# Summing wrapped spectra by accumulating transfers into DRAM, and one doubling step by accumulating transfers into SBUF, in a two-layer SSM and SwiGLU kernel

## The chip, the cores and the metric

The kernel runs on one core of a Trainium2 chip. The metric is the device time of one launch in microseconds: 1188.11 us, median of three runs. The engines are written as in the profile: PE (TensorE matmul), PEld (its weight loads), DVE (VectorE), ACT (ScalarE), POOL (GpSimd) and SP (SyncE, which here only issues transfers). Each engine works through its own queue in order.

## The reference, cut to what matters

One sequence of 2048 rows and 512 channels passes twice through an S4 convolution layer and a SwiGLU layer, each on the layer-normed input and added back.

```python
logdA = dt * A                                   # A complex [512, 128], dt = exp(log_dt)
P = jnp.exp(logdA[:, :, None] * l[None, None, :])            # 128 complex powers for 2048 lags
K = jnp.einsum("dn,dnl,dn->dl", Cc, P, dB).real              # the convolution kernel [512, 2048]
Kf = rfft(pad(K, 2048)); Uf = rfft(pad(u, 2048))
y  = irfft(Uf * Kf)[:2048] + u * Dskip

x = x + ssm(layernorm(x)); x = x + ((silu(n @ w_gate) * (n @ w_up)) @ w_down)   # twice; n = layernorm(x)
```

## The kernel before

The program has three stages.

**The kernel of the convolution** (0 to about 310 us). The 512 channels go in eight chunks of 64. For a chunk, the lag is split in two digits. `gen_g` makes `g`, the coefficients C·dt·B times the powers 0 to 31, real and imaginary in `g[:, 0]` and `g[:, 1]`, by doubling: powers 1 to 3, then 4 to 7 from 0 to 3, 8 to 15 from 0 to 7, 16 to 31 from 0 to 15. A doubling is a complex product: two DVE products into `g` and a scratch tile (`tm`, named `btl` in the profile; `th_`, named `tmp`) and a sum of them. For 4 and 8 the sums are DVE subtractions and additions (L488, L489). For 16 they are transfers that POOL issues and that add into SBUF (`accum_op=OP.add`, L494 and L499). `gen_turns`, `gen_reduce`, `gen_trig` (phases and sines: L365, L385, L388 on DVE, L376, L382, L395 to L397 on ACT), `gen_exp` and `gen_mags` (magnitudes) and `gen_e` (their products: L450 to L459 on DVE) make the other digit's table `re`, `im` of the chunk after the next. `lags` contracts both on PE (L509, L510) into `pk`, ACT copies it to `ks` (L515), `spread` turns it on PE into `kp` (L525), ACT copies that to `kt` (L1001), and `spectra` transforms `kt` on PE (L546) for four frequency classes `q` in the order 0, 3, 1, 2 and four blocks `k` of 512 lags. Between them PE sums squares of the weight matrices (L320, from ACT's L316).

In `spectra`, the spectrum of block k wraps into block k+1 by a turn of ±90 degrees, so what is stored for k = 1 to 3 is s[i, k] ± s[1−i, k−1], with i the real or imaginary part. ACT copies the product out of PSUM (`s1`, L555), POOL copies block 0 to `w0r` (L557) and makes the two sums (`wo`, L563), and SP writes three blocks to DRAM (`wdr`, L569). For the last three classes blocks 1 to 3 are made later than block 0 (L566, L567), after the work that starts the next stage.

**The hand-over** (about 310 to 350 us): the first convolution block is finished on DVE, its norm goes over POOL (L204 to L207), ACT and PE, the last three spectra are made, the weights are split into two halves of fp16 (ACT L626, DVE L632, L654) and the first SwiGLU matmuls start.

**The blocks** (to the end): eight blocks of 512 rows, each a convolution (DVE L736 and L739, which read `w` from `wdr` and `uu` from `udr`; PE L270, L755) and a SwiGLU (PE L860 to L862, L874 to L876).

In the first stage and the hand-over up to the second convolution block, PE, DVE and ACT run in the order in which the program is written: generators of instructions are advanced one step at a time by `take(generator, steps)`, and the numbers in these calls set the order. The queues of POOL and SP, and everything after that, are ordered by a scheduler when the program is built. Buffers come from named pools; the tag `uu` has three buffers and holds `s1`, the `u` of the second block and `uu`; the tag `sg` has two and holds `wo` and later the SwiGLU's `sg`.

Of the kernel before, what the change touches and what calls it, by code (L numbers as in the profile page):

```python
# [15 lines left out]
AF = mybir.ActivationFunctionType  # L16
OP = mybir.AluOpType
# [5 lines left out]
P = 128  # L23
T = 512
NB = L // T
# [9 lines left out]
DC = 64  # L35
# [46 lines left out]
def kernel(ctx, tc, x, a_re, a_im, b_re, b_im, c_re, c_im, log_dt, d_skip,  # L82
                           w_gate, w_up, w_down, c_ef, c_ei, c_ek, c_am, c_eh, c_eih, out):
    nc = tc.nc
# [10 lines left out]
    def tl(shape, name, tag, dt=F32):  # L95
        return sb.tile(shape, dt, name=name, tag=tag, bufs=BUFS[tag])
# [365 lines left out]
    def gen_g(ch, ts, g):  # L462

        re, im, mu, xz, mz, t16 = ts
        w_ = w0[:, :, ch * DC:(ch + 1) * DC]
        for t in xz:
            V.tensor_tensor(t, t, mz, OP.mult)
        yield
        tm, th_ = tmp
        V.tensor_tensor(g[:, :, 0], w_, re[:, :, 64].unsqueeze(1).to_broadcast([P, 2, DC]), OP.mult)  # L470
        V.tensor_tensor(tm[:, :, 0], w_[:, ::-1], im[:, :, 64].unsqueeze(1).to_broadcast([P, 2, DC]), OP.mult)
        yield
        V.tensor_tensor(g[:, 0, 0], g[:, 0, 0], tm[:, 0, 0], OP.subtract)
        V.tensor_tensor(g[:, 1, 0], g[:, 1, 0], tm[:, 1, 0], OP.add)
        yield
        zr, zi = (t[:, :3].unsqueeze(1).to_broadcast([P, 2, 3, DC]) for t in xz)
        V.tensor_tensor(g[:, :, 1:4], g[:, :, 0:1].to_broadcast([P, 2, 3, DC]), zr, OP.mult)
        V.tensor_tensor(tm[:, :, :3], g[:, ::-1, 0:1].to_broadcast([P, 2, 3, DC]), zi, OP.mult)
        yield
        V.tensor_tensor(g[:, 0, 1:4], g[:, 0, 1:4], tm[:, 0, :3], OP.subtract)  # L480
        V.tensor_tensor(g[:, 1, 1:4], g[:, 1, 1:4], tm[:, 1, :3], OP.add)
        for n in (4, 8):
            yield
            zr, zi = (t[:, ZP.index(n)].unsqueeze(1).unsqueeze(1).to_broadcast([P, 2, n, DC]) for t in xz)
            V.tensor_tensor(g[:, :, n:2 * n], g[:, :, 0:n], zr, OP.mult)
            V.tensor_tensor(tm[:, :, :n], g[:, ::-1, 0:n], zi, OP.mult)
            yield
            V.tensor_tensor(g[:, 0, n:2 * n], g[:, 0, n:2 * n], tm[:, 0, :n], OP.subtract)  # L488
            V.tensor_tensor(g[:, 1, n:2 * n], g[:, 1, n:2 * n], tm[:, 1, :n], OP.add)  # L489
        yield  # L490
        zr, zi = (t[:, NZ - 1:].to_broadcast([P, 16, DC]) for t in xz)
        V.tensor_tensor(g[:, 1, 16:], g[:, 1, :16], zr, OP.mult)
        V.tensor_tensor(th_, g[:, 0, :16], zi, OP.mult)
        G.dma_start(g[:, 1, 16:], th_, accum_op=OP.add)  # L494
        yield
        tl_ = tm.rearrange("p i s d -> p (i s) d")
        V.tensor_tensor(g[:, 0, 16:], g[:, 0, :16], zr, OP.mult)
        V.scalar_tensor_tensor(tl_, g[:, 1, :16], -1.0, zi, OP.mult, OP.mult)
        G.dma_start(g[:, 0, 16:], tl_, accum_op=OP.add)  # L499
        yield  # L500
# [30 lines left out]
    def spectra(ch, kt, k0, k1, qs=QORD):  # L531
# [4 lines left out]
        for q in qs:  # L536
# [6 lines left out]
            for i, c in [(i, c) for c in range(4) for i in range(2)] if k1 == 1 else \  # L543
# [3 lines left out]
                if k0 == 1 and (i, c) == (0, 3):  # L547
                    yield
            yield
            if k1 == 1:  # L550
                A.activation(w0r[:, h, q, :, off:off + DC].rearrange("p i (g d) -> p i g d", g=4), pw[:, :, 0], AF.Copy)
                yield
                continue
            s1 = tl([P, 2, NB, 4, 16], "s1", "uu")
            A.activation(s1[:, :, :nk], pw, AF.Copy)  # L555
            if k0 == 0:
                G.tensor_copy(w0r[:, h, q, :, off:off + DC].rearrange("p i (g d) -> p i g d", g=4), s1[:, :, 0])  # L557
            sp, np_ = s1, NB - 1
            wo = tl([P, 2, NB - 1, 4, 16], "wo", "sg")
            ops = (OP.subtract, OP.add) if q % 2 == 0 else (OP.add, OP.subtract)  # L560
            for i in range(2):
                if k0 == 0:
                    G.tensor_tensor(wo[:, i], s1[:, i, 1:], s1[:, 1 - i, :3], ops[i])  # L563
                else:
                    w0s = w0r[:, h, q, 1 - i, off:off + DC].rearrange("p (g d) -> p g d", g=4)
                    G.tensor_tensor(wo[:, i, 0], s1[:, i, 0], w0s, ops[i])  # L566
                    G.tensor_tensor(wo[:, i, 1:], s1[:, i, 1:3], s1[:, 1 - i, :2], ops[i])  # L567
            for k in range(1, NB):
                nc.sync.dma_start(wdr[k, h, q, :, :, off:off + DC].rearrange("p i (g d) -> p i g d", g=4),  # L569
                                  wo[:, :, k - 1])  # L570
            yield


    def sizes(ch, kt, junk):

# [19 lines left out]
    def take(it, n):  # L595
        for _ in range(n):
            next(it, None)
# [301 lines left out]
    with tc.manual_schedule(engines={mybir.EngineType.Activation, mybir.EngineType.DVE, mybir.EngineType.PE}):  # L899
# [58 lines left out]
        for i in range(NCH - 1):  # L958
# [24 lines left out]
            if more:  # L983
                rd = gen_reduce(ts[i + 2])
                next(rd)
            for g in (gg, gg, ge, gg, ge, gg, gg, rd, rd, ge, rd, rd, ge, rd, rd, rd, rd):
                take(g, 1)
            while tops:
                tops.pop(0)()
# [3 lines left out]
            if more:  # L993
                f = second(*sec[i])
                next(f)
            take(gg, 2)
            if more:
                tr = gen_trig(ts[i + 2])
                take(tr, 1)
# [93 lines left out]
        take(rest, 3)  # L1093
        take(second(*sec[-1], space=pbig), 2)
        take(rest, 100)
        split(1, 0)
        take(first, 1)
        split(0, 1)
# [47 lines left out]
```

## Time and profile before

| | |
|---|---|
| median of three runs | 1188.11 us (1188.05 to 1190.89) |
| the profiled execution, its own time | 1194.56 us |
| its span, first to last instruction | 1192.8 us |
| PE busy | 1108.3 us (93%) |
| DVE busy | 1026.5 us (86%) |
| ACT busy | 618.0 us (52%) |
| POOL busy | 185.0 us (16%) |
| mean granted TensorE clock | 0.983 |

A busy share over the whole span mixes the three stages. In the first stage POOL is far from idle and PE, DVE and ACT are all close to full; in the last, PE and DVE are. The program has one core, so there is one row of clock and span.

### The profile page before, as it was taken

The numbers are of one execution on the slowest core, as the hardware profiler recorded it, in microseconds if no ns is written. First come the engines' busy times: TensorE is split into PE (matmuls) and PEld (weight loads), VectorE is DVE, ScalarE is ACT, GpSimd is POOL, SyncE is SP. The second block draws the span as 40 slices with busy tenths as digits, with TensorE's granted clock in tenths as the row PEclk, the third lists the DMA queues.
The fourth block names the chain that finished last, engine by engine and source line by source line (L and its number), as shares of the span: only waits on it lengthen the run. The fifth ranks groups of instructions, "written<-read, shape, count | busy, mean of one in ns | idle before, by whom it ended". The sixth has DMA issues, their size and how long they took to land.

```text
span 1192.8 us, 25266 instructions
## 1 busy us (share of the span) xinstructions
PE 1108.3 (93%) x10268; PEld 861.2 (72%) x10268; DVE 1026.5 (86%) x1621; ACT 618.0 (52%) x1166; POOL 185.0 (16%) x238
## 2 busy tenths in 40 slices
PE   2889999889887989999999999999999999999998
PEld 2767776667875767768677787868687686867875
DVE  7989999997879999999999999999992899983211
ACT  6998887862355544537743523655432553224211
POOL 3105454343310011202100000211000010000000
PEclk9989999999989999999999999999999999999999
DMA  6444445577497326432344354324434134312000
GB/s 234 141 107 127 114 119 127 126 181 201 141 297 221 109 89 163 161 111 89 85 152 146 115 165 142 111 81 150 140 123 133 45 115 128 125 46 45 15 23 18
DMA packets 139031, 147.95 MB, mean 124 GB/s; under 512 B 77921, under 2 KB 87137, under 8 KB 138914
## 3 DMA queue, kind: packets, MB, share of 16 engines
q1 hardware_dynamic: 134050, 129.56, 35.8%
q0 software_dynamic: 4864, 16.78, 5.9%
q8 instruction: 80, 1.31, 0.5%
q14 instruction: 37, 0.30, 0.1%
HBM read 99.24 MB, written 28.31 MB: 107 GB/s over the span
## 4 chain that ended last, share of the span: by engine, by line
PE 35%; DVE 26%; issue 5%; ACT 3%; DMA 2%; POOL 2%; SPq 1%; DVEq 0%; ACTq 0%; POOLq 0%
PE pgu L860 6%; PE pgu L861 6%; PE pgu L862 6%; DVE t L736 4%; PE py L874 4%; PE py L875 4%; PE py L876 3%; DVE yk L739 3%; DVE yk L736 3%; PE pi L755 3%; PE pf L270 2%; DVE z L226 2%; DVE sg L866 2%; POOL rs L221 2%; DVE bt L226 1%
## 5 line engine op out<-in xcount | busy, mean ns | idle before, releaser
L860 PE MATMUL pgu<-mix,wsl 128*128 128x256 f16 x1280 | 350.2, 274 | 5.3 <-DVE sg L866 3.6
L862 PE MATMUL pgu<-mix,wsl 128*128 128x256 f16 x1280 | 350.3, 274 | 3.6 <-DVE wsl L632 3.6
L861 PE MATMUL pgu<-mix,wsl 128*128 128x256 f16 x1280 | 350.2, 274 | 0.0
L874 PE MATMUL py<-wsl,hh 128*128 128x512 f16 (+1 forms) x352 | 135.5, 385 | 8.9 <-DVE sgr L836 3.1
L861 PEld LDWEIGHTS <-wsl 128*128 128x128 f16 x1280 | 125.7, 98 | 21.8 <-issue 5.8
L862 PEld LDWEIGHTS <-wsl 128*128 128x128 f16 x1280 | 125.7, 98 | 19.1 <-DVE wsl L632 3.9
L860 PEld LDWEIGHTS <-wsl 128*128 128x128 f16 x1280 | 125.7, 98 | 15.8
L876 PE MATMUL py<-wsl,hl 128*128 128x512 f16 (+1 forms) x352 | 135.2, 384 | 1.3 <-DVE hl L868 1.3
L865 ACT ACTIVATE sg<-pgu,sc 128x512 f32<-128x512 f32 x80 | 54.5, 682 | 135.4 <-PE pgu L862 116.5
L736 DVE TENSOR_TENSOR t<-uu,w 128x1024 f32<-128x1024 f32 x96 | 117.0, 1219 | 8.2 <-DMA uu<-udr 7.9
L875 PE MATMUL py<-wsl,hh 128*128 128x512 f16 x320 | 123.3, 385 | 0.0
L739 DVE TENSOR_TENSOR yk<-yk,t 128x1024 f32<-128x1024 f32 x96 | 116.9, 1218 | 0.2
L866 DVE SCALAR_TENSOR_TENSOR sg<-pgu,sc,sg 128x512 f32<-128x512 f32 x80 | 59.7, 746 | 51.0 <-ACT sg L865 50.8
L546 PE MATMUL pw<-kt,ek 128*128 128x256 f32 (+2 forms) x420 | 98.6, 373 | 0.0
L755 PE MATMUL pi<-yl,mix 128*128 128x256 f16 x672 | 91.4, 273 | 1.7 <-ACT yl L744 1.4
L546 PEld LDWEIGHTS pw<-kt,ek 128*128 128x128 f32 x420 | 78.7, 195 | 9.5
L867 ACT ACTIVATE hh<-sg 128x512 f16<-128x512 f32 x80 | 50.0, 625 | 57.5 <-DVE sg L866 57.4
L221 POOL TENSOR_TENSOR rs<-mv,mhalf 128x2 f32<-128x2 f32 (+1 forms) x21 | 38.3, 1824 | 263.2 <-ACT mv L220 255.8
L270 PE MATMUL pf<-z,eh 128*128 128x256 f16 x576 | 74.6, 273 | 1.4 <-ACT z L260 1.4
L755 PEld LDWEIGHTS <-mix 128*128 128x128 f16 x672 | 65.2, 98 | 13.0 <-issue 2.0
L736 DVE TENSOR_TENSOR yk<-u,w0r 128x1024 f32<-128x1024 f32 x56 | 68.2, 1218 | 0.3 <-ACT u L272 0.3
L875 PEld LDWEIGHTS <-hh 128*128 128x128 f16 (+1 forms) x352 | 34.8, 99 | 46.2 <-issue 11.7
(240 smaller groups left out, 2245.8 us busy)
## 6 DMA issues: line engine op xcount, KB each, us to landing
w<-wdr SPq DMA_DIRECT2D x96, 256.0 KB, 2.7
uu<-udr SPq DMA_DIRECT2D x96, 256.0 KB, 3.0
udr<-u POOLq DMA_DIRECT2D x32, 256.0 KB, 2.9
wdr<-wo SPq DMA_DIRECT2D x96, 64.0 KB, 2.5
udr<-u SPq DMA_DIRECT2D x16, 256.0 KB, 2.2
g<-tmp POOLq DMA_DIRECT2D x8, 512.0 KB, 4.5
g<-btl POOLq DMA_DIRECT2D x8, 512.0 KB, 5.9
n<-ndr SPq DMA_DIRECT2D x16, 256.0 KB, 3.0
```

The lines of the kernel that those rows point to most:

```text
L270: PE.matmul(pf[:, o], lhsT=e, rhs=m, start=k == 0, stop=k == len(terms) - 1)
L546: PE.matmul(pw[:, i], lhsT=e, rhs=kt[:, :, c + 4 * k0:4 * k1:4, :].rearrange("p g k d -> p k g d"), start=c == 0, stop=c == 3)
L736: V.tensor_tensor(t, uu.unsqueeze(1).to_broadcast([P, 2, 2, HD]), w.unsqueeze(2).to_broadcast([P, 2, 2, HD]), OP.mult)
L739: V.tensor_tensor(yk, yk, t, OP.add)
L755: PE.matmul(pi[:, o], lhsT=e, rhs=m, start=k == 0, stop=k == len(terms) - 1)
L860: PE.matmul(o, lhsT=wgu(wi, k, 0)[:, fs], rhs=nh[:, k], start=k == 0, stop=False)
L861: PE.matmul(o, lhsT=wgu(wi, k, 0)[:, fs], rhs=nlo[:, k], start=False, stop=False)
L862: PE.matmul(o, lhsT=wgu(wi, k, 1)[:, fs], rhs=nh[:, k], start=False, stop=k == 3)
L866: V.scalar_tensor_tensor(sg, pgu[:, 1], sc6[:, 4:5], sg, OP.mult, OP.mult)
L874: PE.matmul(py[:, r], lhsT=hh[:n, f, rc], rhs=wd(f, 0)[:n], start=f == 0, stop=False)
L875: PE.matmul(py[:, r], lhsT=hh[:n, f, rc], rhs=wd(f, 1)[:n], start=False, stop=False)
L876: PE.matmul(py[:, r], lhsT=hl[:n, f, rc], rhs=wd(f, 0)[:n], start=False, stop=f == FT - 1)
```

## The change

Four edits.

1. In `gen_g` the step from 8 to 16 powers loses its two DVE sums. Its two DVE products of 1024 elements become four of 512, one of them with a factor −1, and two transfers issued by POOL add the second products into `g` (L488, L491 of the changed kernel).
2. In `spectra`, POOL computes nothing. ACT writes a negated copy `ng` of one part (L572, or L570 from `s1`) beside `s1`. SP copies block 0 from `s1` to `w0r` (L573) and writes the unwrapped blocks 1 to 3 of both parts to `wdr` (two transfers, L576). Then POOL issues two transfers that add `ng` and `s1`, one block further, into the same places of `wdr` (L585, L586). They are put in the program one class later, by `wrapped(1)`; each has to wait until the plain write of its place has landed. For the three late classes block 0 is copied back from `w0r` by ACT (L569).
3. The `take` order of a chunk: the doubling to 16 powers now stands before the phase reduction, one step of `gen_e` behind it, and the last doubling before `spread` instead of behind it.
4. Behind the last spectra stands `wrapped()`, for the last two additions.

`ng` takes the place of `wo` in tag `sg` (two buffers). `s1` is now also read by the second addition, so its buffer comes free later.

The diff:

```diff
@@ gen_g
         for n in (4, 8):
             yield
             zr, zi = (t[:, ZP.index(n)].unsqueeze(1).unsqueeze(1).to_broadcast([P, 2, n, DC]) for t in xz)
+            if n == 8:
+                V.tensor_tensor(g[:, 1, 8:16], g[:, 1, :8], zr[:, 1], OP.mult)
+                V.tensor_tensor(tm[:, 1], g[:, 0, :8], zi[:, 1], OP.mult)
+                G.dma_start(g[:, 1, 8:16], tm[:, 1], accum_op=OP.add)
+                V.tensor_tensor(g[:, 0, 8:16], g[:, 0, :8], zr[:, 0], OP.mult)
+                V.scalar_tensor_tensor(tm[:, 0], g[:, 1, :8], -1.0, zi[:, 0], OP.mult, OP.mult)
+                G.dma_start(g[:, 0, 8:16], tm[:, 0], accum_op=OP.add)
+                continue
             V.tensor_tensor(g[:, :, n:2 * n], g[:, :, 0:n], zr, OP.mult)
             V.tensor_tensor(tm[:, :, :n], g[:, ::-1, 0:n], zi, OP.mult)
@@ spectra
+            w0s = w0r[:, h, q, :, off:off + DC]
+            wrapped(1)
             if k1 == 1:
-                A.activation(w0r[:, h, q, :, off:off + DC].rearrange("p i (g d) -> p i g d", g=4), pw[:, :, 0], AF.Copy)
+                A.activation(w0s.rearrange("p i (g d) -> p i g d", g=4), pw[:, :, 0], AF.Copy)
                 yield
                 continue
-            s1 = tl([P, 2, NB, 4, 16], "s1", "uu")
-            A.activation(s1[:, :, :nk], pw, AF.Copy)
-            if k0 == 0:
-                G.tensor_copy(w0r[:, h, q, :, off:off + DC].rearrange("p i (g d) -> p i g d", g=4), s1[:, :, 0])
-            wo = tl([P, 2, NB - 1, 4, 16], "wo", "sg")
-            ops = (OP.subtract, OP.add) if q % 2 == 0 else (OP.add, OP.subtract)
+            s1 = tl([P, 2, NB, DC], "s1", "uu")
+            ng = tl([P, NB - 1, DC], "ng", "sg")
+            j = q % 2
+            A.activation(s1[:, :, k0:].rearrange("p i k (g d) -> p i k g d", g=4), pw, AF.Copy)
+            if k0:
+                A.activation(s1[:, :, 0], w0s, AF.Copy)
+                A.activation(ng, s1[:, 1 - j, :3], AF.Copy, scale=-1.0)
+            else:
+                A.activation(ng.rearrange("p k (g d) -> p k g d", g=4), pw[:, 1 - j, :3], AF.Copy, scale=-1.0)
+                nc.sync.dma_start(w0s, s1[:, :, 0])
+            to = wdr[1:, h, q, :, :, off:off + DC].rearrange("k p i d -> p i k d")
             for i in range(2):
-                (the sums on POOL: L563, or L566 and L567)
-            for k in range(1, NB):
-                nc.sync.dma_start(wdr[k, h, q, :, :, off:off + DC].rearrange("p i (g d) -> p i g d", g=4),
-                                  wo[:, :, k - 1])
+                nc.sync.dma_start(to[:, i], s1[:, i, 1:])
+            wraps.append((to[:, j], ng, to[:, 1 - j], s1[:, j, :3]))
             yield
 
+    wraps = []
+
+    def wrapped(keep=0):
+        while len(wraps) > keep:
+            t0, f0, t1, f1 = wraps.pop(0)
+            G.dma_start(t0, f0, accum_op=OP.add)
+            G.dma_start(t1, f1, accum_op=OP.add)
@@ the loop over chunks
-            for g in (gg, gg, ge, gg, ge, gg, gg, rd, rd, ge, rd, rd, ge, rd, rd, rd, rd):
+            for g in (gg, gg, ge, gg, gg, gg, gg, rd, rd, ge, rd, rd, ge, rd, rd, rd, rd, ge):
                 take(g, 1)
...
-            take(gg, 2)
@@ the hand-over
         take(rest, 100)
+        wrapped()
```

The change moves instructions at three places that matter below. The first is DVE in the middle of a chunk: the doubling to 16 powers, the doubling to 32 behind it, and the phase reduction (L388) and the products of `gen_e` (L450, L453). Before:

```order
L453 TENSOR_TENSOR re<-re 128x4x8x32
L388 SCALAR_TENSOR_TENSOR im<-t_1333,re 128x64x2
L388 SCALAR_TENSOR_TENSOR im<-t_1333,re 128x64 x2
L485 TENSOR_TENSOR g<-g,xr 128x2x512
L486 TENSOR_TENSOR btl<-g,xi 128x1024
L488 TENSOR_TENSOR g<-g,btl 128x512
L489 TENSOR_TENSOR g<-g,btl 128x512
L492 TENSOR_TENSOR g<-g,xr 128x1024
```

And with the change, in the same chunk:

```order
L490 SCALAR_TENSOR_TENSOR btl<-g,xi 128x512
L385 TENSOR_TENSOR xi<-xi,xr 128x384
L388 SCALAR_TENSOR_TENSOR im<-t_1335,re 128x64x16
L450 TENSOR_TENSOR im<-im,re 128x4x8x32
L388 SCALAR_TENSOR_TENSOR im<-t_1335,re 128x64x8
L388 SCALAR_TENSOR_TENSOR im<-t_1335,re 128x64x4
L453 TENSOR_TENSOR re<-re 128x4x8x32
L388 SCALAR_TENSOR_TENSOR im<-t_1335,re 128x64x2
L388 SCALAR_TENSOR_TENSOR im<-t_1335,re 128x64 x2
L453 TENSOR_TENSOR re<-re 128x4x8x32
L500 TENSOR_TENSOR g<-g,xr 128x1024
```

L490 is the last of the four products of the step to 16 powers and L500 the first reader of what the two transfers add. The step moved ahead of the phase reduction, which stands, with an L450 and two L453, between the two. In the first chunk only one L388 stands there.

The second is POOL at the hand-over, where L204 to L207 are the norm of the first SwiGLU block. Before:

```order
L567 TENSOR_TENSOR wo<-s_3349 128x128
L566 TENSOR_TENSOR wo<-s_3349,w0r 128x64
L567 TENSOR_TENSOR wo<-s_3349 128x128
L204 TENSOR_SCALAR rs<-mv 128x2
L205 TENSOR_TENSOR rs<-rs,mhalf 128x2
```

And with the change:

```order
L586 DMA wdr<-s_3248 128x3x64
L585 DMA wdr<-ng 128x3x64 x2
L586 DMA wdr<-s_3363 128x3x64
L204 TENSOR_SCALAR rs<-mv 128x2
L205 TENSOR_TENSOR rs<-rs,mhalf 128x2
```

Where the sums of one class stood ahead of L204, there are now two transfers of that class (the second L585 and the last L586), each of which waits for the landing of a plain write.

The third is DVE right after it: L632 (L646 with the change) makes the low halves of the weights, L736 (L750) is the first product of the second convolution block and needs `uu`, L222 is the norm of the next rows and needs a POOL result. Before:

```order
L632 SCALAR_TENSOR_TENSOR wsl_3093<-xg,sc_93,wsl_3092 128x2x344
L736 TENSOR_TENSOR t<-uu,w 128x1024
L632 SCALAR_TENSOR_TENSOR wsl_3094<-st_3470,sc_93,wsl_3093 128x4x344
L739 TENSOR_TENSOR yk<-yk,t 128x1024
L632 SCALAR_TENSOR_TENSOR wsl_3092<-st_3483,sc_93,wsl_3092 128x2x344
L632 SCALAR_TENSOR_TENSOR wsl_3093<-st_3483,sc_93,wsl_3092 128x2x344
L632 SCALAR_TENSOR_TENSOR wsl_3094<-st_3487,sc_93,wsl_3093 128x4x344
```

And with the change:

```order
L646 SCALAR_TENSOR_TENSOR wsl_3105<-xg,sc_93,wsl_3104 128x2x344
L646 SCALAR_TENSOR_TENSOR wsl_3106<-st_3483,sc_93,wsl_3105 128x4x344
L646 SCALAR_TENSOR_TENSOR wsl_3104<-st_3496,sc_93,wsl_3104 128x2x344
L646 SCALAR_TENSOR_TENSOR wsl_3105<-st_3496,sc_93,wsl_3104 128x2x344
L222 SCALAR_TENSOR_TENSOR rs<-mv,rs 128x2
L646 SCALAR_TENSOR_TENSOR wsl_3106<-st_3500,sc_93,wsl_3105 128x4x344
L750 TENSOR_TENSOR t<-uu,w 128x1024
```

The first read of `uu` moved behind four of these weight instructions and behind L222. On PE the order up to the hand-over is the same as before.

7 lines of the change are left out of this document (removed).

## The prediction

> **What bounds the kernel now.** The removed work lies in the first 345 us, so I read that stage first: busy time by stretches cut at ACT's `ks` (L515), which begins each chunk's turn.
>
> ```profile
> core 0: us, PE busy (x) PEld busy (x) DVE busy (x) ACT busy (x) POOL busy (x), PEclk, DMA share, GB/s
> 98.88:130.27 31.39, 28.37 (x391) 21.75 (x390) 30.46 (x38) 26.46 (x43) 13.65 (x19) 1.00 0.56 132
> 161.30:193.96 32.66, 29.75 (x391) 23.08 (x390) 32.52 (x40) 26.20 (x44) 16.09 (x20) 0.95 0.56 138
> ```
>
> DVE is busy for 97% of the one turn and 99.6% of the other, which looks like the bound. The waits over the five turns from 98.88 to 256.34 (total, times, longest) say otherwise:
>
> ```profile
> ACT ks L515 <- PE pk L510: 15.4, 5, 3.5
> PE nrm L320 <- ACT sq L316: 8.3, 5, 1.7
> DVE xi L385 <- ACT xr L376: 0.4, 1, 0.4
> ```
>
> ACT and PE wait for each other once in every turn; neither waits for DVE, and DVE waits for ACT. One turn in order of time, ACT and then PE:
>
> ```profile
> 193.96 1.02 ACT L515 ACTIVATE ks<-pk 128x1024 f32<-128x1024 f32 x1 [2.98 <-PE pk L510]
> 199.00 0.57 ACT L555 ACTIVATE s<-pw 128x512 f32<-128x512 f32 x1
> 213.31 1.23 ACT L316 ACTIVATE sq<-st 128x344 bf16<-128x344 f32 x3
> 213.83 1.07 PE L320 MATMUL nrm<-sq,onesb 128*128 128x344 bf16 x3 [1.64 <-ACT sq L316]
> 225.38 1.03 ACT L515 ACTIVATE ks<-pk 128x1024 f32<-128x1024 f32 x1 [3.49 <-PE pk L510]
> ```
>
> From `ks` to the first `sq` ACT shows no idle time (193.96 to 213.31, 19.4 us); from `nrm` to the end of the lag products PE waits for nothing but its own issue (213.83 to 225.38, 11.5 us); then `ks` again. That loop of ACT and PE is the 31.4 us of the turn, and no DVE instruction is in it. DVE keeps pace beside it. Behind the first stage the picture turns:
>
> ```profile
> 346.00:360.00 14.00, 14.00 (x112) 11.75 (x111) 14.00 (x21) 8.92 (x13) 0.00 (x0) 0.85 1.04 320
> 400.00:500.00 100.00, 94.69 (x791) 74.81 (x790) 98.29 (x169) 54.94 (x108) 14.62 (x13) 0.98 0.45 135
> ```
>
> There DVE is full and PE has gaps, so what DVE loses or gains at the hand-over is kept.
>
> **The change part by part.** The sum is made as a difference in the profiled execution (1194.56 us, span 1192.8) and put on the median, 1188.11, which is 6.4 lower; every term is a stretch of well under 10 us, so the half per cent between the two doesn't touch it.
>
> *DVE relief, in the turns.* Mean nanoseconds over the five turns, then two undisturbed records from the quiet start:
>
> ```profile
> L485 DVE TENSOR_TENSOR g<-g,xr 128x1024 f32<-128x1024 f32 x5 | 6.5, 1296 | 0.0
> L485 DVE TENSOR_TENSOR g<-g,xr 128x512 f32<-128x512 f32 x5 | 3.5, 699 | 0.0
> L488 DVE TENSOR_TENSOR g<-g,btl 128x512 f32<-128x512 f32 x5 | 3.5, 692 | 0.2
> L489 DVE TENSOR_TENSOR g<-g,btl 128x512 f32<-128x512 f32 x5 | 3.4, 684 | 0.0
> L467 DVE TENSOR_TENSOR xi<-xi,mzp 128x384 f32<-128x384 f32 x5 | 4.4, 875 | 0.0
> L450 DVE TENSOR_TENSOR im<-im,re 128x1024 f32<-128x1024 f32 x10 | 13.9, 1394 | 0.0
> 25.73 0.55 DVE L467 TENSOR_TENSOR xi<-xi,mzp 128x384 f32<-128x384 f32 x1
> 31.86 1.22 DVE L450 TENSOR_TENSOR im<-im,re 128x1024 f32<-128x1024 f32 x1
> ```
>
> Two sums go (0.69 + 0.68 = 1.38), two products of 1.3 become four of 0.70 (+0.2): DVE saves 1.2 us a turn. With POOL's sums gone the stretched instructions shrink as well; these two lines alone give 0.33 + 2 × 0.17 = 0.7 us a turn. Ten to fifteen us of DVE time go in all. I price this at **0**: the cover is the loop of ACT and PE. If that were not the bound, it would be worth up to PE's wait of 1.7 us a turn (first rival). The Trainium skill, page "SBUF — State Buffer", section "Who interferes with whom", says that a DVE instruction with two SBUF inputs contends with a GpSimd instruction that reads SBUF, and that PE and ACT never wait on anyone; the stretched rows agree with the first half, and by the second half the loop gets nothing from a silent POOL, so the sum stays as it is.
>
> *The negated copy on ACT.* No copy of 192 elements from PSUM is in the trace; the nearest are
>
> ```profile
> L551 ACT ACTIVATE w0r<-pw x3: 277/277/277, 301.4 to 304.9; 128x128 f32<-128x128 f32 x3
> L555 ACT ACTIVATE s<-pw x32: 490/588/610, 88.3 to 330.5; 128x512 f32<-128x512 f32 x29, 128x384 f32<-128x384 f32 x3
> ```
>
> so 0.28 to 0.49, by the slope 0.33, of which neighbouring ACT records overlap by 0.1: 0.23 us. Of the four per turn only the one behind L555 at 199.00 stands between `ks` and `sq`; the other three eat into the wait of 3 us before `ks`. Five turns: **+1.2 us** (bounds 0.9 to 2.5).
>
> *The first chunk.* Here only one L388 stands between the step to 16 powers and L500, and DVE has to wait for two transfers. The nearest prices:
>
> ```profile
> L690 POOL DMA_DIRECT2D udr<-u x32: 539/542/672, 421.9 to 876.2; - x32
> L499 POOL DMA_DIRECT2D g<-btl x8: 861/870/882, 50.9 to 269.8; - x8
> udr<-u POOLq DMA_DIRECT2D x32, 256.0 KB, 2.9
> g<-tmp POOLq DMA_DIRECT2D x8, 512.0 KB, 4.5
> 51.30 1.12 ACT L395 ACTIVATE re<-im 128x1024 f32<-128x1024 f32 x1 [1.06 <-DVE im L388]
> ```
>
> An addition of 256 KB into SBUF should land 2.9 (a plain one of that size) to 4.5 us after its issue; I take 3.5, nearer the plain one. From L490 to L501 DVE has 1.1 + 1.1 us to do, so it waits some 1.8 us in two pieces, less the 1.2 saved: the last L388 comes 0.6 later, and ACT, which waits for it at 51.30 and is full from there, moves with it. **+0.7 us** (0 to 2.5). In later chunks some 7 us stand in between.
>
> *The hand-over.* DVE before:
>
> ```profile
> 341.38 1.22 DVE L736 TENSOR_TENSOR t<-uu,w 128x1024 f32<-128x1024 f32 x1 [7.94 <-DMA uu<-udr]
> 342.52 1.64 DVE L632 SCALAR_TENSOR_TENSOR wsl<-st,sc,wsl 128x1376 f16<-128x1376 f32 x1
> 345.22 3.34 DVE L632 SCALAR_TENSOR_TENSOR wsl<-st,sc,wsl 128x688 f16<-128x688 f32 x3
> 344.22 0.40 PE L862 MATMUL pgu<-mix,wsl 128*128 128x256 f16 x1 [3.62 <-DVE wsl L632]
> 344.00:350.00 6.00, 5.78 (x28) 4.10 (x29) 6.00 (x9) 0.00 (x0) 0.00 (x0) 0.50 1.05 404
> ```
>
> DVE stood for 7.94 us at a load of `uu` with four ready L632 behind it; PE stood 3.62 us for one of them and then ran 6 us at a granted clock of 0.50. With the read of `uu` behind them, the first three can go into the gap. The fourth is behind L222, whose POOL step was at 341.5 to 343.2, so it comes about where the first is now. Against it stands POOL's L204:
>
> ```profile
> 319.48 0.78 POOL L204 TENSOR_SCALAR rs<-mv 128x2 f32<-128x2 f32 x1 [1.99 <-DVE mv L203]
> 314.61 0.49 ACT L555 ACTIVATE s<-pw 128x384 f32<-128x384 f32 x1 [2.49 <-PE pw L546]
> wdr<-wo SPq DMA_DIRECT2D x96, 64.0 KB, 2.5
> ```
>
> It now follows two transfers that wait for plain writes of the copy of 314.61: issued at 315.2 and 316.1, landed 2.5 to 3.2 later, then two POOL issues of about 1.2 (384 rows of 256 B; bounds 0.54, the plain 256 KB, and 1.9): L204 at about 320.8, 1.3 late. DVE by 344: of the four L632, all done with the change instead of one, so 1.64 + 2 × 0.85 = 3.3 us gained, with that delay already in it. **−3.3 us** (bounds −6.6, PE's stall and the half clock with it, to +3 if POOL comes late).
>
> Sum: +1.2 + 0.7 − 3.3 = −1.4: **1186.7 us**.
>
> **The rivals.**
>
> *DVE is the bound after all*: it is over 97% busy, and its one short wait could be noise. Then each turn falls by PE's wait of 1.7 us, over six turns 10 us, and with the hand-over the time is 1176 to 1178. Against it: ACT's rows show no wait for DVE in any of the five turns.
>
> *Slower: the copy buffer.* `ng` has two buffers, and a class needs the buffer of the class before last.
>
> ```profile
> 213.81 2.50 SPq L314 DMA_DIRECT2D st<-in_B_w_up_dram  x3
> 214.44 0.58 ACT L555 ACTIVATE s<-pw 128x512 f32<-128x512 f32 x1
> 220.17 0.59 ACT L555 ACTIVATE s<-pw 128x512 f32<-128x512 f32 x1
> 220.65 1.24 ACT L316 ACTIVATE sq<-st 128x344 bf16<-128x344 f32 x3
> ```
>
> The first class is copied at 214.44; SP is free at 216.3, its first plain write is out at 217.8 and down at 219.4 to 220.3, the addition lands 3.5 later (2.3 to 5.9): 222.9, at worst 226. The third class wants the buffer at 220.7 and ACT then needs 1.24 for `sq` before `ks` at 225.4. So up to 224.1 it is hidden, and each us beyond is one on the loop. It decides from an addition of 4.7 us on. At 5.9, 1.4 us a turn; with PE's longer waits pulling the clock down in some turns (the turn with 0.95 is 1.3 us longer than the one with 1.00), 2 to 2.5: 1188.1 + 5 × 2.2 − 1.4, about 1198. For it: pieces of 256 B, read, added and written in DRAM, of which no row exists. The Trainium skill, "DMA: Bandwidth & Descriptors", section "Specifications", puts line rate at 512 B and above. The rows agree: 64 KB in 256 B pieces took 2.5 us, 256 KB in longer ones 2.9.
>
> *The hand-over gains nothing*: `uu` now sits behind a 768 KB load in SP's queue, L222 behind POOL's transfers; the 3.3 goes to 0 to +3, the time to 1190 to 1193.
>
> *The last stage falls otherwise*: its order is made anew by the scheduler, DVE and PE are both near full, and PE's waits there come in pieces of 1 to 3.5 us; a few of them more or fewer move the end by ±4.
>
> **How the numbers follow.** What this kernel's measurement can tell from no change is 0.3%, 3.6 us: 1184.5 to 1191.7. The forecast with its own bounds (1184 to 1191) 0.45; DVE as the bound 0.15, faster; the copy buffer 0.17, slower; no gain at the hand-over 0.11, half of it slower; the last stage 0.12, half faster and half slower. Out of the forecast's own 0.45, 0.09 lies beyond 3.6 us on the fast side, where PE's half clock goes too. Faster 0.15 + 0.06 + 0.09 = 0.30; slower 0.17 + 0.05 + 0.06 = 0.28; same 0.42. Range 1177 to 1198, from DVE as the bound to the copy buffer.
>
> **What would show it.** Right: turns of 31 to 32 us as before; DVE's idle time up by 2 to 4 us a turn, put down to ACT (L385 waiting for L376); ACT's wait before `ks` shorter by about 1 us, PE's before `nrm` longer by 0.2; in the first chunk DVE waiting at L500 and L501 for transfers; PE without a wait for `wsl` near 342 and full clock there. Wrong: turns under 30.5 us (DVE was the bound); ACT's L572 waiting for a transfer, with `ks` no longer waiting for PE (copy buffer); DVE waiting 5 us or more at L222 or L750.

## The result and the profile after

The changed kernel takes 1217.96 us (median of 6 runs, 1216.51 to 1220.61) against 1190.33 us for the kernel before (6 runs beside it): 1.0237 times as long, 95% interval 1.0219 to 1.0256. The forecast was 1186.7 us with a range of 1177 to 1198, so it is wrong in its sign and its range.

The stages, cut at ACT's `ks` (L515, now L523). "SwiGLU" is the first matmul of L860 (L874). The second profile of the kernel before was taken among the experiments; it matters, because the first one was of a long execution.

| us | before, as quoted in the prediction | before, second profile | changed |
|---|---|---|---|
| its own time | 1194.56 | 1186.43 | 1216.51 |
| first `ks` | 68.65 | 68.26 | 69.31 |
| first to seventh `ks`, six turns | 187.69 | 187.98 | 194.99 |
| seventh turn | 26.16 | 25.78 | 32.15 |
| eighth `ks` to SwiGLU | 51.17 | 48.67 | 52.68 |
| SwiGLU to the end | 859.1 | 853.9 | 865.6 |

Every stage is longer. The turns of the changed kernel, by stretches from `ks` to `ks`:

```profile
core 0: us, PE busy (x) PEld busy (x) DVE busy (x) ACT busy (x) POOL busy (x), PEclk, DMA share, GB/s
100.41:134.82 34.41, 29.72 (x389) 22.50 (x388) 27.23 (x39) 27.48 (x48) 14.54 (x15) 0.95 1.06 165
198.86:230.52 31.66, 28.12 (x391) 21.88 (x390) 27.05 (x39) 27.20 (x49) 14.25 (x14) 1.00 1.09 180
264.30:296.45 32.15, 24.74 (x370) 19.81 (x369) 19.06 (x30) 9.00 (x18) 14.35 (x13) 0.95 1.03 217
```

DVE is indeed relieved: 27 us busy in a turn instead of 31. The turn is not shorter, and where the clock (PEclk) is 0.95 it is longer by 2 to 3 us. The share of the DMA engines went from 0.5 to over 1. The waits up to 345 us (total, times, longest):

```profile
POOL wdr L585 <- DMA wdr<-s: 96.5, 11, 15.2
DVE xi L385 <- ACT xr L376: 20.1, 6, 5.1
ACT ng L572 <- DMA wdr<-ng: 18.6, 6, 8.4
DVE g L500 <- DMA g<-btl: 12.6, 2, 11.1
PE pk L517 <- DMA g<-btl: 10.2, 2, 5.2
```

DVE's new idle time is put down to ACT, as forecast. But ACT waits for a copy buffer, DVE for the step to 16 powers, PE for the last doubling, all of them for transfers that POOL issues; and POOL itself stands 96.5 us before L585, for plain writes of SP. The seventh turn shows how these belong together. DVE, then POOL, PE and ACT:

```profile
259.38 0.69 DVE L487 TENSOR_TENSOR btl<-g,xi 128x512 f32<-128x512 f32 x1
275.79 1.22 DVE L500 TENSOR_TENSOR g<-g,xr 128x1024 f32<-128x1024 f32 x1 [11.11 <-DMA g<-btl]
...
265.69 1.28 POOL L586 DMA_DIRECT2D wdr<-s  x1 [3.96 <-ACT ks L523]
266.48 1.42 POOL L488 DMA_DIRECT2D g<-btl  x1
267.83 2.31 POOL L491 DMA_DIRECT2D g<-btl  x1
278.97 1.28 POOL L585 DMA_DIRECT2D wdr<-ng  x1 [8.83 <-DMA wdr<-s]
...
289.38 0.45 PE L517 MATMUL pk<-re,g 128*32 128x64 f32 x3 [5.05 <-DMA g<-btl]
...
295.60 0.34 ACT L572 ACTIVATE ng<-pw 128x192 f32<-128x192 f32 x1 [8.40 <-DMA wdr<-ng]
```

L488's data were ready at 260.1, but it stands in POOL's queue behind an L586 that waits, and is issued at 266.5, 6.4 us late; then it takes 9.3 us to land. DVE has nothing else to do in this chunk and waits 11.11 us for it. So the last doubling is late too, and PE stands 5.05 us for it. The additions themselves wait for plain writes (8.83 us at one L585), and with them the buffer that ACT needs (8.40 us). For the L586 at 265.69 (and the L585 at 335.09 below) the profile names an instruction of ACT that ended in the same moment; but a plain write of SP landed at 265.14 (334.54), and POOL starts 0.54 to 0.57 us behind such a landing at 25 of the 27 transfers of L585 and L586 that it stood for. At the hand-over the same happens to L204, whose input was ready at 332.9, and PE then stands 5.74 us (3.33 and 2.96 before):

```profile
335.09 1.28 POOL L585 DMA_DIRECT2D wdr<-ng  x1 [12.97 <-ACT s L567]
337.75 0.19 POOL L204 TENSOR_SCALAR rs<-mv 128x2 f32<-128x2 f32 x1
340.25 1.97 PE L815 MATMUL pt<-ident,nn 128*128 128x128 f32 x8 [5.74 <-ACT nn L813]
```

The loss behind the hand-over is of another kind. SP, then PE:

```profile
466.11 0.39 SPq L232 DMA_DIRECT2D n<-xdr  x1
466.56 0.50 SPq L232 DMA_DIRECT2D xg<-xdr  x1
467.15 2.13 SPq L829 DMA_TRANSPOSE mix<-nn  x1
...
477.53 0.26 PE L843 MATMUL pgu<-wsl,mix 128*128 128x96 f16 x1 [8.10 <-DMA mix<-nn]
```

The scheduler now puts two loads of 1 MB just ahead of a transpose that PE needs next; it lands 10.3 us after its issue; the median of these transposes is 2.5. In the kernel before these two loads stood behind that block's transposes (472.68 and 473.15, transposes to 470.27), and PE's longest wait for `mix` was 3.39 us (3.62 in the second profile).

### The profile page after: what moved, and what is told of

It reads as the page before. It is cut to its first block, busy times and chain, and to the rows that moved or that the text cites. A ratio compares the mean times of both kernels' runs of the same rounds, so it can differ in the third digit from the quotient of the medians.

```text
span 1214.7 us, 25337 instructions
## 1 busy us (share of the span) xinstructions
PE 1110.6 (91%) x10268; PEld 863.8 (71%) x10268; DVE 998.4 (82%) x1621; ACT 625.5 (51%) x1201; POOL 202.1 (17%) x219
## 3 DMA queue, kind: packets, MB, share of 16 engines
q0 software_dynamic: 32768, 27.27, 16.0%
## 4 chain that ended last, share of the span: by engine, by line
PE 30%; DVE 29%; ACT 14%; issue 13%; DMA 8%; POOL 4%; SPq 1%; DVEq 0%; POOLq 0%; ACTq 0%
DVE t L750 4%; PE pgu L874 4%; PE pgu L876 4%; PE pgu L875 4%; PE pw L554 3%; DVE yk L753 3%; POOL rs L221 3%; DVE z L226 3%; PE py L888 3%; PE py L889 3%; PE py L890 3%; PE pi L769 2%; DVE yk L750 2%; DMA wdr<-s 2%; DVE sg L880 2%
## 5 line engine op out<-in xcount | busy, mean ns | idle before, releaser
L874 PE MATMUL pgu<-mix,wsl 128*128 128x256 f16 x1280 | 350.0, 273 | 6.7 <-DVE sg L880 5.7
L874 PEld LDWEIGHTS <-wsl 128*128 128x128 f16 x1280 | 125.6, 98 | 16.9 <-issue 0.7
L750 DVE TENSOR_TENSOR t<-uu,w 128x1024 f32<-128x1024 f32 x96 | 117.0, 1219 | 1.0 <-DMA uu<-udr 0.7
L221 POOL TENSOR_TENSOR rs<-mv,mhalf 128x2 f32<-128x2 f32 (+1 forms) x21 | 51.2, 2440 | 216.9 <-ACT mv L220 216.8
L585 POOL DMA_DIRECT2D wdr<-ng x32 | 55.9, 1748 | 135.8 <-DMA wdr<-s 105.2
L758 ACT ACTIVATE yl<-mix,sy 128x512 f16<-128x512 f32 x56 | 40.2, 717 | 59.5 <-DVE mix L755 59.3
```

The lines of the kernel that those rows point to most:

```text
L221: G.tensor_tensor(rs[:, :rows], mv[:, :rows, 1], mhalf[:, :rows], OP.pow)
L750: V.tensor_tensor(t, uu.unsqueeze(1).to_broadcast([P, 2, 2, HD]), w.unsqueeze(2).to_broadcast([P, 2, 2, HD]), OP.mult)
L874: PE.matmul(o, lhsT=wgu(wi, k, 0)[:, fs], rhs=nh[:, k], start=k == 0, stop=False)
```

## The experiments

All of them at a glance: ratio to the kernel before with its 95% interval, median, and from one profile the eighth `ks` (282.5 and 282.0 before), the seventh turn (26.2, 25.8), the stretch to SwiGLU (51.2, 48.7) and from there to the end (859.1, 853.9). The medians of the kernel before beside them were 1189.6 to 1191.4. The profiles of copies_alone and pool_writes_elsewhere are of their fastest executions, 8.9 and 5.8 us below the median.

| kernel | ratio | median | eighth `ks` | seventh turn | to SwiGLU | to the end |
|---|---|---|---|---|---|---|
| changed | 1.0237 (1.0219 to 1.0256) | 1217.96 | 296.45 | 32.15 | 52.68 | 865.6 |
| spectra_alone | 1.0156 (1.0125 to 1.0186) | 1208.98 | 296.91 | 31.93 | 53.88 | 856.9 |
| doubling_alone | 1.0073 (1.0053 to 1.0092) | 1199.57 | 285.14 | 26.95 | 51.92 | 859.2 |
| no_accumulation | 1.0114 (1.0085 to 1.0143) | 1204.32 | 292.30 | 25.92 | 49.44 | 860.5 |
| four_copy_buffers | 1.0250 (1.0218 to 1.0283) | 1220.50 | 295.70 | 33.71 | 53.44 | 869.3 |
| plain_pool_writes | 1.0189 (1.0164 to 1.0213) | 1213.90 | 293.20 | 30.43 | 51.64 | 868.0 |
| pieces_of_768 | 1.0120 (1.0089 to 1.0150) | 1206.22 | 295.53 | 31.06 | 49.96 | 858.9 |
| pool_writes_elsewhere | 1.0090 (1.0059 to 1.0121) | 1199.36 | 287.30 | 26.31 | 48.29 | 856.2 |
| copies_alone | 1.0068 (1.0046 to 1.0089) | 1200.27 | 286.88 | 26.02 | 48.80 | 853.9 |
| copies_alone_2 (one run) | | 1198.88 | 291.65 | 25.97 | 50.15 | 855.3 |
| late_fourth_copy | 0.9995 (0.9967 to 1.0022) | 1188.36 | 283.69 | 25.85 | 49.95 | 855.2 |
| doubling_in_the_middle | 0.9999 (0.9973 to 1.0025) | 1191.76 | 283.26 | 26.08 | 51.18 | 859.4 |
| both_sides_relieved | 0.9995 (0.9964 to 1.0026) | 1192.91 | 283.45 | 27.27 | 50.32 | 858.3 |

### The two halves

My theory after the result: POOL's transfers into DRAM hold up everything else that POOL issues. The rival: the moved step to 16 powers loses by itself.

```diff
# spectra_alone: the change without edits 1 and 3
-            if n == 8:
-                (four products and two transfers)
# doubling_alone: the kernel before with edits 1 and 3 only
+            if n == 8:
+                (four products and two transfers)
```

> The changed spectra with the old doubling to 16 powers and the old take order. Places: the eighth ks (282.5 us before, 296.5 with the change) and the time. Theory 'POOL's transfers': the accumulating transfers into DRAM fill POOL's transfer queue, so the copy buffer and the last doubling's sums come late; then this half alone carries most of the loss: eighth ks at 288 to 294, ng still waiting for a landing in most turns, time 1202 to 1215. Rival 'the moved step to 16 powers': the loss comes from the step's transfers, which DVE must wait for in the first and the last chunk; then this half is near the kernel before: eighth ks at 282 to 286, time 1187 to 1195.

> The step to 16 powers by transfers and the new take order, with the spectra summed on POOL as before. Theory 'POOL's transfers': nothing fills the queue, so the sums land in 3 to 4.5 us and the last chunk's wait at L500 is under 4 us (11.1 with the whole change): eighth ks at 282 to 287, time 1186 to 1194. Rival 'the moved step': the wait in the last chunk stays at 8 us or more, eighth ks at 288 or later, time 1195 to 1205.

In the median the halves add up: 18.6 and 9.2 us over before make 27.8, the change 27.6. By stages they don't, so this is in part chance: up to the eighth `ks` the spectra alone lose as much as the whole change (296.91 against 296.45), and the stall of 8.10 us for `mix` stands in neither half. The spectra carry two thirds of the total and the whole loss of the seventh turn, without the step being moved at all. The step carries the rest, which the theory did not expect; L500 does not wait there, L501 waits 4.9 us once.

### Taking the additions away

```diff
# no_accumulation (the wrapped part is left out of the spectra)
-            G.dma_start(t0, f0, accum_op=OP.add)
-            G.dma_start(t1, f1, accum_op=OP.add)
```

> The changed kernel without the two accumulating transfers per class: the plain writes and the negated copies stay, the wrapped part is left out of the spectra. Theory 'POOL's transfers': the waits of ng vanish, the sums of g land as before (4.5 and 5.9 us instead of 6.4 and 6.9), L204 is not late, eighth ks at 281 to 286, time 1183 to 1196, with what the last stage's new order costs still in it. Rival 'the moved step': L500 in the last chunk still waits 8 us or more, eighth ks at 288 or later.

The seventh turn is back at 25.9 us and the stretch to SwiGLU at 49.4, so both losses come from these transfers. The eighth `ks` (292.30) and the time (1204.32) did not come back as far as expected. Some 6 us of that are one turn of 37.70 us, in which one POOL instruction that takes 0.3 to 0.9 us in the other profiles lasted 10.19 us (least, median and most of three, in ns). It ran from 141.69 to 151.88; DVE was busy without a pause up to 151.73, but whether DVE held it is not shown. The sums of `g` stood behind it in POOL's queue: L502 was issued at 154.66, 9.5 us after its data were ready.

```profile
L423 POOL CAST mzp<-rho x3: 515/602/10191, 10.9 to 141.7; 128x128 bf16<-128x128 f32 x3
```

### The prediction's slower rival: two copy buffers

```diff
# four_copy_buffers: two copies packed in one buffer of 2 KB
-            ng = tl([P, NB - 1, DC], "ng", "sg")
+            if len(ngs) % 2 == 0: ngs.append(tl([P, 2, NB - 1, DC], "ng", "sg"))
+            else: ngs.append(ngs[-1])
+            ng = ngs[-1][:, (len(ngs) - 1) % 2]
```

> The changed kernel with two negated copies packed in each buffer, so that four stand at once and a class waits for the landing of the copy three classes before. If the two buffers are what the change loses by (the prediction's slower rival, alone), ng's waits (18.6 us in all) go and the eighth ks comes 5 us or more earlier than 296.5, time 1205 to 1212. If POOL's transfers are simply late, the waits move on to s1's buffers and to the sums of g: eighth ks within 3 us of 296.5, time 1214 to 1219.

No gain at all: the eighth `ks` is 0.75 us earlier. The waits of `ng` are gone, L500 in the last chunk still waits 8.7 us and PE 6.3 us for the last doubling. ACT's wait for its buffer is a symptom of the late transfers, not the cause.

### Adding, small pieces, or waiting

Three properties of these transfers could make them late: they add, they come in pieces of 256 B, or they wait, at the head of POOL's queue, for the plain write of the same place. The Trainium skill, "DMA: Bandwidth & Descriptors", section "Rules for kernel authors", demands that wait: an accumulating transfer may not run beside another access of the same bytes. The traces show the wait; no run here adds without it. One experiment for each:

```diff
# plain_pool_writes (writes over instead of adding)
-            G.dma_start(t0, f0, accum_op=OP.add)
+            G.dma_start(t0, f0)
# pieces_of_768
-    wdr = dram.tile([NB, 2, 4, P, 2, HD], F32, name="wdr")
+    wdr = dram.tile([2, 4, P, 2, 4, NB - 1, DC], F32, name="wdr")
# pool_writes_elsewhere: as plain_pool_writes, into wd2, which nothing else writes
-            wraps.append((to[:, j], ng, to[:, 1 - j], s1[:, j, :3]))
+            wraps.append((t2[:, j], ng, t2[:, 1 - j], s1[:, j, :3]))
```

> The changed kernel with the same POOL transfers into DRAM in the same places, but writing instead of adding, so the wrapped sum is left out of the spectra. It keeps the waits for the plain writes, the order of POOL's queue and the number of pieces, and takes away only the adding. If the adding in DRAM is slow: landings of these transfers fall from 4.5 and 5.1 us to about 3, those of g's sums from 6.4 and 6.9 to 4.5 and 5.9, the seventh turn (eighth ks less seventh) from 32.2 to 27 or less, time 1200 to 1207. If the order of the queue and the waits in it are the cause: the seventh turn stays at 30 or more, time 1212 to 1219.

> The changed kernel with the spectra laid out in DRAM so that a partition's three blocks of one part lie together: plain writes and additions go in pieces of 768 B instead of 256 B (and the loads of w in the last stage in pieces of 256 B instead of 1 KB, so only the first stage counts here). If the pieces of 256 B are what makes the queue slow: the additions land in 3.5 us or less, the seventh turn falls to 28 or less, the eighth ks to 287 to 291, and POOL issues each in under 1.0 us (1.28). If the waits in the queue are the cause: the eighth ks stays at 294 to 298.

> As plain_pool_writes, but into DRAM that nothing else writes, so that these transfers no longer wait for the plain writes; number, size and pieces are the same, and the wrapped sum is left out of the spectra. If it is that wait, at the head of POOL's in-order queue with g's sums behind it, that makes the last chunk late: no wait at L500 in the last chunk beyond 3 us, ng's waits gone, seventh turn 26 to 27.5 (30.4 with plain writes, 25.9 without the transfers), eighth ks at 287 to 290. If the load of the transfers themselves does it: seventh turn 29.5 to 31.

First what the transfers themselves cost: duration of POOL's issue (least, median, most, in ns) and time to landing, in the changed kernel, with plain writes, and in pieces of 768 B:

```profile
L585 POOL DMA_DIRECT2D wdr<-ng x32: 1268/1294/2882, 93.9 to 351.8; - x32
DMA to landing us min/median/max: 3.4/4.5/10.8
```

```profile
L585 POOL DMA_DIRECT2D wdr<-ng x32: 757/771/1137, 95.5 to 347.7; - x32
DMA to landing us min/median/max: 2.2/3.2/7.9
```

```profile
L585 POOL DMA_DIRECT2D wdr<-ng x32: 857/871/1921, 94.3 to 349.3; - x32
DMA to landing us min/median/max: 2.7/4.2/8.5
```

Adding costs 0.5 us of issue and 1.3 us of landing, and large pieces give back most of the issue. Neither moves the first stage much: the seventh turn stays above 30 us in both, and the eighth `ks` comes 3.3 and 0.9 us earlier. Now without the wait: POOL in the same chunk (lines are one or two higher than in the changed kernel: L489, L492, L503 and L508 are the sums of `g`), DVE's L501, and the turn:

```profile
259.14 0.92 POOL L489 DMA_DIRECT2D g<-btl  x1 [0.66 <-DVE btl L488]
260.34 0.86 POOL L492 DMA_DIRECT2D g<-btl  x1 [0.28 <-DVE btl L491]
270.10 0.92 POOL L503 DMA_DIRECT2D g<-tmp  x1 [2.71 <-DVE tmp L502]
272.36 0.86 POOL L508 DMA_DIRECT2D g<-btl  x1 [1.34 <-DVE btl L507]
...
265.13 1.22 DVE L501 TENSOR_TENSOR g<-g,xr 128x1024 f32<-128x1024 f32 x1 [1.69 <-DMA g<-btl]
...
260.99:287.30 26.31, 23.18 (x370) 18.29 (x368) 20.45 (x32) 8.89 (x17) 8.17 (x11) 1.00 0.99 267
```

Every sum of `g` is now issued right behind DVE's product (the wait in brackets is POOL's for DVE). L501, the reader of the first, starts at 265.13, 6.0 us after the issue instead of 9.3. The seventh turn is 26.3 us, the waits of `ng` come to 0.6 us in all, and the time falls by 14.5 us from plain_pool_writes (13.2 when each is taken against the kernel before that ran beside it). The transfers are as many and as large in both, and the DMA engines are no less busy in this turn (0.99 against 0.88 with plain writes and 1.03 in the changed kernel). So **the wait at the head of POOL's in-order queue** is the cause in the seventh turn and at the hand-over. The order of POOL's queue changed too, since the scheduler makes it anew, and the two aren't separated. The slow landing of that sum goes with the wait in the main: 9.3 us in the changed kernel, 8.0 with plain writes, 6.0 here.

Part of the 14.5 us is indirect. Of the 21 us between the spans of the two profiles 5.9 lie before the eighth `ks`, 3.4 at the hand-over and 11.8 behind it. The stall of 8 us behind the two loads of 1 MB stands in the changed kernel, four_copy_buffers (8.68) and plain_pool_writes (8.22), in none of the others; these three have 865.6 to 869.3 us from SwiGLU to the end, all others 853.9 to 860.5. Only in these three does SP's queue have the transpose directly behind the two loads. That order is the scheduler's, made anew for each kernel. pieces_of_768 gained its 11.7 us there and at the hand-over, and 0.9 us up to the eighth `ks`.

### The price of the copies

```diff
# copies_alone: the kernel before, with ACT's copy into unused space
+            ng = wt[:, 384:480].bitcast(BF16).rearrange("p (k d) -> p k d", k=NB - 1)
+            if k0 == 0:
+                A.activation(ng.rearrange(...), pw[:, 1 - q % 2, :3], AF.Copy, scale=-1.0)
```

> The kernel before with only ACT's negated copy added for the 29 classes of the chunks, into unused space, read by nothing. The prediction's term: 0.23 us a turn, eighth ks 1.2 to 1.6 us later than before, time 1188 to 1192. If PE's longer wait before nrm (1.6 to 1.95 us) also pulls the clock to half more often: three of the five middle turns with a clock of 0.95 and about 1.6 us longer each, eighth ks 3 to 6 us later, time 1192 to 1197.

> The kernel with the copies alone, for a second profile, since the first was the fastest of its ten runs (1191.4; median 1200.3). Expected: a time near 1200, and 8 us more than in the first profile to be found as windows at half clock (1.7 us each) and as a wait at the hand-over, not as longer turns of ACT.

> The kernel before, unchanged, for a second profile: how far the stages of one profiled execution repeat. Expected: ks starts within 2 us of the first profile's, the span between 1186 and 1193, a clock of 0.95 in none to two of the five middle turns.

The second profile of the kernel before has a span of 1184.6 us, just under the expected range; its `ks` starts lie within 1.3 us of the first profile's. The copies cost 9.4 us in the median of ten runs (1191.4 to 1202.8), eight times the 1.2 us of the prediction's term and above both ranges that were expected. Three turns of the second profile of the copies:

```profile
100.34:133.90 33.56, 28.89 (x386) 21.79 (x385) 31.17 (x40) 27.35 (x48) 11.35 (x17) 0.95 0.55 136
166.91:199.44 32.53, 29.31 (x397) 22.99 (x396) 31.20 (x41) 27.11 (x48) 15.99 (x14) 1.00 0.41 92
199.44:232.79 33.35, 28.66 (x385) 21.66 (x385) 32.06 (x41) 27.06 (x48) 17.63 (x18) 0.95 0.50 118
```

Its five middle turns average 33.1 us (31.5 in the first profile of before), four of them with a clock of 0.95. That was not expected: longer turns, not only half clock and a wait at the hand-over. Half clock comes in stretches of 3.4 us, now and then two or three in a row. One of the changed kernel, in steps of 1 us:

```profile
121.00:122.00 1.00, 0.85 (x5) 0.29 (x3) 0.39 (x1) 1.00 (x4) 0.00 (x0) 1.00 0.38 52
122.00:123.00 1.00, 1.00 (x4) 0.64 (x3) 1.00 (x3) 0.87 (x3) 0.00 (x0) 0.65 0.95 306
123.00:124.00 1.00, 1.00 (x4) 0.82 (x3) 1.00 (x2) 1.00 (x4) 0.00 (x0) 0.50 0.92 258
124.00:125.00 1.00, 1.00 (x4) 0.73 (x3) 1.00 (x4) 1.00 (x3) 0.00 (x0) 0.50 0.82 182
125.00:126.00 1.00, 1.00 (x4) 0.86 (x3) 0.97 (x4) 0.14 (x2) 0.00 (x0) 0.65 0.56 134
```

The shares add up to 0.35 + 0.5 + 0.5 + 0.35 = 1.7 us lost, 3.4 us at half clock. Added up over the span, 11.9 us are lost in the second profile of before, 20.5 in the first and 25.7 in the changed kernel: 8.6 us of clock between two executions of the same kernel whose spans differ by 8.2. Over all profiles, a middle turn (the second to the sixth) has such a stretch in 7 of 30 turns without the copies (six profiles) and in 25 of 45 with them (nine); PE's wait before `nrm` is 1.6 to 1.7 us in the kernel before and 1.9 to 3.1 with the copies.

What sets off half clock can be read from the traces. All changes of the clock fall on a grid of 3.413 us, which lies differently against the turns in each execution. Two pairs of neighbouring windows of that grid, from the first profile of the kernel before:

```profile
148.73:152.14 3.41, 1.85 (x9) 1.15 (x9) 3.41 (x3) 3.06 (x7) 1.61 (x2) 1.00 1.02 190
152.14:155.56 3.42, 3.42 (x20) 2.57 (x22) 3.42 (x7) 2.09 (x4) 3.42 (x1) 1.00 0.98 222
179.45:182.86 3.41, 1.54 (x8) 0.84 (x7) 3.41 (x3) 3.06 (x9) 1.25 (x2) 1.00 1.02 184
182.86:186.27 3.41, 3.41 (x10) 2.70 (x9) 3.41 (x5) 2.46 (x4) 3.41 (x5) 0.50 1.01 207
```

In the first pair PE was busy for 1.85 of 3.41 us and kept its clock; in the second for 1.54, and the next window ran at half. In the fifteen profiles, between 95 and 1180 us, 71 windows at full clock had PE busy for less than 0.4 of the window, and half clock followed all of them; between 0.4 and 0.6 it followed 25 of 128, from 0.6 up none of 4452. So PE's wait once in a turn costs its clock when enough of it, with PE's other gaps, falls into one window: with 1.6 to 1.7 us seldom, with 1.9 and more often. The Trainium skill, "TensorE: Matmul & The Clock Gate", "Part 1: The HAM clock gate", has the same length, a free-running window of about 3.4 us, but asks for a whole idle window; here one that was idle for six tenths was enough every time.

Half clock is not all of the price. Over the runs, by their mean granted clock, 20.0 us are lost with the copies and 16.1 in the kernel before beside them, so at most some 4 of the 9.4 us are clock. The turns at full clock are longer too, 31.7 us with the copies and 31.2 without (means of 20 and 23 turns of all profiles), which is twice the 0.23 us of the forecast.

### Is it the loop of ACT and PE that sets the turn?

```diff
# late_fourth_copy: the kernel before
-            take(sp, 1)
+            spo = sp if more else iter(())          # (and take(sp, 1) in the last chunk)
                 norm_units(3, 9)
+                take(spo, 1)
# doubling_in_the_middle
-            if n == 8:
+            if n == 8 and 0 < ch < NCH - 1:
# both_sides_relieved: the two together
```

> The kernel before with one thing moved: in every turn ACT's copy of the fourth class (0.58 us, the only one between ks and the first sq) goes behind the first sq, where ACT waits for PE anyway. If the loop of ACT and PE sets the turn, as the prediction has it, each of the six full turns falls by 0.5 us and PE's wait before nrm from 1.6 to about 1.1 us: eighth ks at 278.5 to 279.5 (282.0 and 282.5 before). If that wait also decides how often PE falls to half clock, fewer windows at half clock than before in the turns, time 1182 to 1188. If DVE sets the turn (97% busy), nothing moves: eighth ks at 281.5 to 283, time 1188 to 1192.

> doubling_alone (1199.6 us, 9 over before), but with the step to 16 powers by transfers only in chunks 1 to 6; chunks 0 and 7, where no other work of DVE covers the landing, keep the old step and order. If the two uncovered chunks carry the loss: eighth ks at 281 to 284 and time 1187 to 1193. If the six covered chunks lose too, through PE's waits and half clock: time 1195 or more.

> doubling_in_the_middle and late_fourth_copy together: in chunks 1 to 6 DVE has some 2 us less and ACT 0.5 us less between ks and the first sq. If DVE and ACT are two bounds of the same height in the turn, so that relieving one alone gives nothing, both together give about 0.5 us in each of five or six turns: turns at full clock of 30.3 to 30.8 us (31.0 to 31.4), eighth ks 2 to 3 us before that of doubling_in_the_middle, time 1184 to 1188. If something else sets the turn (PE's own 28 us and its waits), the two kernels agree within 1.5 us at the eighth ks.

None of the three differs from before. In late_fourth_copy three middle turns at full clock take 30.30, 31.07 and 31.13 us (30.82 to 31.75 before), two at 0.95 take 33.20 and 33.86. PE's wait before `nrm` fell in four of the five (to 0.78 to 1.33 us), and yet half a microsecond off ACT's part of the loop, 2 us off DVE, and both together give nothing; the theory of two bounds of one height fell too. In both_sides_relieved PE's unexplained waits (for "issue") before L517 and L518 come to 10.1 us between 60 and 300 us (8.7 and 8.2 in the profiles of before); what holds PE there stays open, and with it what sets the turn. doubling_in_the_middle does settle one thing: in the median the covered chunks cost nothing, so the 9.2 us of doubling_alone come from chunks 0 and 7, where nothing covers the landing. By the eighth `ks` only 1.9 us of that can be seen; the rest isn't located. No version beat the kernel before.

## Why the prediction was wrong, point by point

The step that failed is that the text priced POOL's queue at L204 alone: that an addition waiting for SP's plain write holds up whatever POOL issues behind it stands in no term. Second to it, the copies were mis-sized and the gain at the hand-over did not come. By stages, against the two profiles of the kernel before:

| us | forecast | measured |
|---|---|---|
| first `ks` | +0.7 | +0.7 and +1.1 |
| six turns | +1.2 | +7.3 and +7.0 |
| seventh turn | 0 | +6.0 and +6.4 |
| eighth `ks` to SwiGLU | −3.3 | +1.5 and +4.0 |
| SwiGLU to the end | 0 (±4) | +6.5 and +11.7 |

- *DVE relief worth nothing: right.* doubling_in_the_middle takes the sums off DVE at 0.9999 (0.9973 to 1.0025), and in the changed kernel DVE's idle time before L385 is 2.7 to 5.1 us in each of the five middle turns, put down to ACT as listed.
- *The premise that ACT and PE alone bound the turn: not confirmed.* It held against a load on ACT (copies_alone) and failed for a relief of ACT (late_fourth_copy).
- *The copy, +1.2 us: mis-sized.* PE's wait before `nrm` grew by 0.3 us (0.2 forecast), but the copies cost 9.4 us alone: the six turns take 192.8 and 197.0 us with nothing but the copies, so they account for what the changed kernel loses there (194.99). At most some 4 of the 9.4 us are clock. The text had the clock in the slower rival and left it out of this term.
- *The first chunk, +0.7 us: right* (first `ks` 69.31 against 68.65 and 68.26). *"In later chunks some 7 us stand in between": wrong for chunk 7*, which has no phase reduction behind the step. There L500 waited 11.1 us.
- *The hand-over, −3.3 us: wrong.* It rested on a wait of 7.94 us of one execution. The text said that the half per cent between that execution and the median "doesn't touch it"; it sat just there. The second profile of before:

```profile
335.33 1.22 DVE L736 TENSOR_TENSOR t<-uu,w 128x1024 f32<-128x1024 f32 x1 [2.86 <-DMA uu<-udr]
338.18 0.28 PE L862 MATMUL pgu<-mix,wsl 128*128 128x256 f16 x1 [0.56 <-DVE wsl L632]
```

  The new order itself did what was listed: in the changed kernel DVE doesn't wait for `uu` nor PE for `wsl`, and PE has its full clock from 344.2. But L204 came 4.8 us late behind the two transfers, not 1.3, and DVE stands 7.17 us for what follows from it (4.34 and 3.73 before).
- *The copy buffer, 1198 us: seen, but not the cause.* The landing was 4.5 to 5.1 us, around the point of 4.7 from which it decides, and ACT waited 18.6 us; four buffers gained nothing. (At 5.9 us the text's own figures give 5.9 − 4.7 = 1.2 us a turn, not 1.4.)
- *What was missing: POOL's queue.* The changed order of POOL, which the document shows, puts transfers that wait for SP's writes ahead of the sums of `g`, which DVE and PE need at once in the last chunk, and ahead of L204. Taken each against the kernel before beside it, that wait, with the orders that the build makes around it, is worth 13.2 us (plain_pool_writes against pool_writes_elsewhere), the adding 4.6 (the change against plain_pool_writes), and what is left 9.8 (pool_writes_elsewhere against before). The copies and the two uncovered chunks are in these 9.8; they cost 9.4 and 9.2 us alone and so are not additive, for a reason that stays open.
- *The last stage, ±4: too narrow.* One transpose behind two loads cost 8.1 us, and the stage took 6.5 to 11.7 us more.
- *The range of the forecast.* The bounds of the three terms add up to −5.7 and +8.0, that is 1182 to 1196 us, not 1184 to 1191.

## What to carry to other kernels

When work moves from an engine to transfers that this engine issues, write its queue out in order and ask of each entry what it waits for and who waits for what stands behind it: a transfer that must wait for another write holds up everything after it, and here more buffers didn't help. A gap in one profile is worth its length only if a second execution shows it; when the profiled execution is longer than the median, the gap is the first thing to doubt. A small load on the engine that another waits for once in every turn can cost several times its length, in part through the clock, while taking as much away need not bring anything.

## What the runs showed of the hardware

Half clock comes in stretches of 3.4 us that lose 1.7 us each, behind a window of that length in which PE was busy for less than about half: behind all 71 windows below 0.4, none of 4452 from 0.6 up. Their number goes with how executions of one kernel differ (8.6 us of it between the two profiles of before, whose spans differ by 8.2). An addition of 96 KB into DRAM in pieces of 256 B occupies POOL for 1.29 us (1.8 behind another) and lands after 4.5 to 5.1; the same transfer as a plain write takes 0.77 us and lands after 3.2 to 3.7, and in pieces of 768 B the addition takes 0.87 us and lands after 4.2. A transpose issued behind two loads of 1 MB landed after 10.3 us (10.3 to 11.2 in the three kernels that have this order); the median is 2.5.
